# Giving out the middle stage's work in other portions, an earlier start for the second batch, and the order of w_in's quarters

## The chip, the core and the metric

The kernel runs on one core of a Trainium2 chip. The metric is the device time of one execution in microseconds (us). The kernel before took 2536.88 us (median of three runs, 2535.14 to 2537.12).

## The reference

```python
X = np.fft.rfft(x, axis=1)                       # x: 8 batches x 3008 x 256
Yr = Xr @ w_r - Xi @ w_i + b_r                   # 256 x 256, on every frequency
Yi = Xr @ w_i + Xi @ w_r + b_i
Yr = np.sign(Yr) * np.maximum(np.abs(Yr) - lam, 0.0)     # lam = 0.01, the same for Yi
y = np.fft.irfft(Yr + 1j * Yi, n=3008, axis=1)
h = y.reshape(24064, 256) @ w_in                 # 256 x 2048
out = np.maximum(0.01 * h, h) @ w_out            # 2048 x 256
```

w_in and w_out are drawn in double precision and are handed over as pairs of 32-bit words, from which the kernel makes its float numbers itself.

## The kernel before

**Tiling.** The length 3008 is 47 x 64, so the transform of a batch is done in matrix products in two passes. `fwd(b)` does the pass over 47 and writes `u_dram`. `mid(b)`, the middle stage, does the pass over 64, the projection with w_r and w_i, the threshold and the first pass back, and writes `v_dram`. `inverse` reads pieces of it (`vin`), does the last pass, and `forms` makes the operands of the MLP from its result. The MLP goes over 24064 tokens in 47 chunks of 512 tokens, with 8 steps (`q`) a chunk. `moe_a` and `moe_b` make the hidden layer with 7 products per block in place of 8 (L99), `moe_o` multiplies by w_out (L652). Behind the first batch, each product is three matmuls over operands split into a high and a low part (`_hi`, `_lo`).

**The middle stage.** It goes over 12 pairs of frequencies per batch. For the pair j:
- `stage_b(j)` (L379): 4 matmuls from the loaded `u`, and the split of the result into `eh` and `el` (L393 to L396).
- `proj(j)`: 6 matmuls with `wr` into one bank (`ps_k`), from which ACT copies `kc` (L415) and POOL makes `kb` (L417); then 6 with `wn` and 6 with `wd` into another (`ps_y`).
- the threshold on DVE (L425 `t`, L426 `c`, L427 `t`), four moves into `zf` on ACT (L431, L435), the split into `zh` on ACT (L442) and `zl` on DVE (L443).
- `stage_g(j)`: 3 matmuls of 512 columns with `gb`, the copy `v` on ACT (L458) and two DMAs to `v_dram` from ACT's queue (L460).

From the second batch on, every bank of these stages comes from a tag of two banks, `psf`, which `inverse` (L524, `psf<-ga,vin`) and `fwd` use too. For the first batch, nothing of the MLP is there to run beside; its middle stage is the startup.

**What sets the order.** `mid` and `fwd` are generators. Each yields how much work it has just given out, as columns of matmul. The main loop (L798 to L816) walks over the half steps of the MLP; before each it asks the streams to reach a share `frac` of their whole work. `Stream.to` (L702 to L715) takes pieces until the work given out reaches that; a yielded None ends the call, so that the next piece comes a half step later at the soonest. For the middle stage of the second batch (`cur == 0`) `frac` stays at zero for the first fifth of the way and then rises to 1. `tc.issue_after(ins)` places what is traced in its block behind `ins` in the issue order of the engine of `ins`; it adds no wait. Within these bounds a list scheduler chooses each engine's order. One middle stage has to end before the first `inverse` that reads it: that reads a mixed piece, whose `vin` tile has a half of the batch before and a half of this one (`v_load`, L509; the other loads are L503).

**The startup.** w_in comes in four quarters. `convert_win(c)` makes one quarter's float numbers (`float64_parts`: ACT L154 and L155, then DVE) and splits them in three casts on ACT (L196) with three subtractions on DVE (L197). It shares ACT and DVE with the first batch's middle stage.

Of the kernel before, what the change touches and what calls it, by code (L numbers as in the profile page):

```python
# [31 lines left out]
def spectral_mlp_kernel(  # L32
# [20 lines left out]
    D = w_r.shape[0]  # L53
# [7 lines left out]
    CS = 512  # L61
# [12 lines left out]
    sync, act, dve, pool = nc.sync, nc.scalar, nc.vector, nc.gpsimd  # L74

    def bank(tag, bufs):
        return ps.tile([P, 512], F32, name=tag, tag=tag, bufs=bufs)

    def products(dst, pairs):

        terms = []
        for l, r in pairs:
            terms += [(l[0], r[0]), (l[0], r[1]), (l[1], r[0])] if len(l) == 2 else [(l[0], r[0])]
        for i, (a, b) in enumerate(terms):
            last = nc.tensor.matmul(dst, a, b, start=(i == 0), stop=(i == len(terms) - 1))  # L85
        return last


    mlp = []
# [11 lines left out]
    def flat(t):  # L101
        return t.rearrange("p a b -> p (a b)")
# [46 lines left out]
    def float64_parts(raw, a, q):  # L149


        wl, wh = raw[:, :, 0], raw[:, :, 1]
        u = a.bitcast(U32)
        act.mul(q, wl, 2.0 ** -52)  # L154
        act.activation(a, wh.bitcast(F32), AF.Abs, scale=2.0 ** 16)  # L155
        dve.tensor_scalar(a, a, F64_MIN * 2.0 ** 16, F64_MAX * 2.0 ** 16, ALU.max, ALU.min)
        dve.tensor_scalar(u, u, 4, 1, ALU.logical_shift_left, ALU.logical_shift_right)
        dve.scalar_tensor_tensor(u, wh, 0x80000000, u, ALU.bitwise_and, ALU.bitwise_or)
        dve.tensor_scalar(wl, u, 0xFF800000, None, ALU.bitwise_and)
        dve.tensor_mul(q, q, wl.bitcast(F32))  # L160
# [3 lines left out]


    NIN = DF // 4
    win_raw = []

    def load_win(c, queues, behind=None):
        if c % 2 == 0:  # L170
# [9 lines left out]
    def convert_win(c):  # L180


        a, q, s = win_tmp
        if c == 3:
            a = sb.tile([P, NH * NIN], F32, name="cva", tag="wout_hi", bufs=1)
        float64_parts(win_raw[c], a, q)
        dve.tensor_add(a, a, q)
        a = a.rearrange("p (j q i m) -> p j q i m", j=NH, q=2, i=2)
        a11, a12, a21, a22 = (a[:, j, :, i] for i in range(2) for j in range(2))
        dve.tensor_add(s[:, 0], a21, a22)  # L190
        dve.tensor_sub(s[:, 2], a11, a21)
        dve.tensor_sub(s[:, 1], s[:, 0], a11)
        dve.tensor_sub(s[:, 3], a12, s[:, 1])
        hi, lo = (w[:, :, 2 * c:2 * c + 2] for w in consts["win"])
        for k, w in ((slice(0, 2), a[:, :, :, 0]), (2, a22), (slice(3, 7), s)):
            act.copy(hi[:, k], w)  # L196
            last = dve.tensor_sub(lo[:, k], w, hi[:, k].bitcast(F32))  # L197
        return last

# [36 lines left out]
    sent, reads, written, turned, turning, thresholded, filled, returned, tied = [], [], [], [], [], [], [], [], []  # L236
# [111 lines left out]
    def mid(b):  # L348
# [13 lines left out]
        def load(j):  # L362
            u = sb.tile([P, 2, D], F32, name="u", tag="u", bufs=3)
            for c in range(2):
                ld = sync.dma_start(u[c * N2:(c + 1) * N2], ud[c, 2 * j:2 * j + 2, :N2, :].rearrange("k n d -> n k d"))
                if b == 0:
                    reads.append(ld)
            u_t[j] = u
# [30 lines left out]
        def proj(j):  # L399

            e = e_t.pop(j)
            ps_k = bank("psf", 2) if b else bank("pso", 2)
            ps_y = None if b else bank("psf", 2)
            for dst, c, w in ((0, 2, "wr"), (0, 1, "wn"), (D, 0, "wd")):
                if c == 1 and b:
                    ps_y = bank("psf", 2)
                with tc.issue_after(mlp[0].ins) if b and c == 2 else nullcontext():
                    products((ps_k if c == 2 else ps_y)[:, dst:dst + D], [
                        (tuple(t[:, a, c, :] for t in e), tuple(t[:, a, :] for t in consts[w]) if b else (consts[w + "32"][0][:, a, :],)) for a in range(NH)
                    ])  # L410
                if c == 2:
                    kc = ps_k[:, :D]
                    if b:
                        kc = sb.tile([P, D + 40], F32, name="kc", tag="kc")[:, :D]
                        act.copy(kc, ps_k[:, :D])  # L415
                    kb = sb.tile([P, 2, D], F32, name="kb", tag="kb", bufs=1)
                    (pool if b else dve).tensor_add(kb, bias, kc.unsqueeze(1).broadcast_to([P, 2, D]))  # L417
                if c:
                    yield 6 * D
                if c == 2 and b and j:  # L420
                    stage_g(j - 1)
                    yield 3 * CS
            t = sb.tile([P, 2, D], F32, name="t", tag="t" if b else "v", bufs=1 if b else 2)
            c = sb.tile([P, 2, D], F32, name="c", tag="kb" if b else "yt", bufs=1)
            dve.tensor_add(flat(t), ps_y, flat(kb))  # L425
            dve.tensor_scalar(c, t, LAMBDA, -LAMBDA, ALU.min, ALU.max)  # L426
            thresholded.append(dve.tensor_sub(t, t, c))  # L427
            zf = z0[j % 3] if b == 0 else sb.tile([P, 2, D], F32, name="zf", tag="zf", bufs=1)
            for i in range(2):
                s = slice(64 * i, 64 * (i + 1))  # L430
                act.copy(zf[:64, i, :], t[s, 0, :])  # L431
                if b == 0 and j == NPAIR - 1:
                    dve.tensor_scalar(zf[64:, i, :], t[s, 1, :], sign[s, NK1 + j:NK1 + j + 1], None, ALU.mult)
                else:
                    act.mul(zf[64:, i, :], t[s, 1, :], sign[s, NK1 + j:NK1 + j + 1])  # L435
            if b == 0:
                z_t[j] = (zf,)
                yield 6 * D
                return
            z = sb.tile([P, 2, 2, D], F32R, name="zh", tag="z", bufs=1)  # L440
            zh, zl = z[:, 0], z[:, 1]
            act.copy(zh, zf)  # L442
            dve.tensor_sub(zl, zf, zh.bitcast(F32))  # L443
            z_t[j] = (zh, zl)
            yield 6 * D

        def stage_g(j):
            pg = bank("psh", 4) if b < 1 else bank("psf", 2)
            with tc.issue_after(filled[0].ins) if b == 0 and filled else nullcontext():
                last = products(pg, [(consts["gb" if b else "gb32"], tuple(flat(z) for z in z_t.pop(j)))])  # L450
            if b == 0:
                turning.append(last)
                tied[:] = [last]
                if NPAIR - 3 <= j < NPAIR - 1:
                    next(fp)
            v = sb.tile([P, 2, D], F32, name="v", tag="v" if b else "y") if b or j < NPAIR - 1 else sb.tile(
                [P, 2, D], F32, name="v", tag="t", bufs=1)
            act.copy(flat(v), pg)  # L458
            for c in range(2):
                put = act.dma_start(vd[c, 2 * j:2 * j + 2, :N2, :].rearrange("k n d -> n k d"), v[c * N2:(c + 1) * N2])  # L460
                if b == 0:
                    returned[:] = [put]
# [4 lines left out]
        if b:  # L467
            for s in range(NPAIR):
                if s + 2 < NPAIR:
                    load(s + 2)  # L470
                with tc.issue_after(mlp[0].ins):
                    stage_b(s)
                yield 16 * P
                yield None
                yield from proj(s)
            stage_g(NPAIR - 1)
            yield 3 * CS
            return
        for s in range(NPAIR + 3):
            if s + 2 < NPAIR:  # L480
# [319 lines left out]
    for i, pos in enumerate(moe()):  # L800
        if i % 2 == 0 and len(converted) < NQ:
            with tc.issue_after(made[0].ins), tc.issue_after(made[1].ins):
                next(wout, None)
        while cur + 1 < NB - 1 and pos >= (read[cur + 1] if cur >= 0 else 0):
            for s in streams:
                s.finish()
            cur += 1
            streams = ([Stream(fwd(cur + 1), (FWD + 4 * CS) * SHARE)] if cur else []) + [mids[cur]]
        frac = (pos - read[cur]) / (read[cur + 1] - read[cur]) if cur + 1 < NB else 1
        if cur == 0:  # L810
            frac = max(0, frac - 0.2) * 1.25
        work = frac / 0.95 * sum(s.total for s in streams)
        with tc.issue_after(converted[-1].ins) if cur == 0 else nullcontext():
            for s in streams:
                s.to(work / s.total)
                work = max(0, work - s.total)  # L816
# [106 lines left out]
```

## Time and profile before

| what | value |
|---|---|
| three runs | 2536.88, 2535.14, 2537.12 us |
| the profiled execution's own time | 2536.06 us |
| its span, first to last instruction | 2534.3 us |
| granted TensorE clock, mean | 0.996 |
| ACT L639, Prelu of 3/4 of a block | 368 times, 847 ns each |
| ACT L603, cast of a block | 376 times, 1050 ns each |

The table's first three rows are three measures of one thing: the execution that was profiled took 2536.06 us, of which 1.8 us lie around the span. A line of the profile reads "line engine operation out<-in"; names are those of the tiles, with buffer numbers left out. PE is TensorE's matmul, ACT is ScalarE, DVE is VectorE, POOL is GpSimd, SP is SyncE, whose queue carries most DMAs. A bracket at the end of a row of a timeline is the time for which the engine stood idle ahead of it, and what ended that.

### The profile page before, as it was taken

Reading aid. Unit: us, or ns where it says so; the run is one execution under the profiler, and the core shown is the slowest. Engines: PE = TensorE matmul, PEld = TensorE weight load, DVE = VectorE, ACT = ScalarE, POOL = GpSimd, SP = SyncE. Lnnn points to the kernel's source line nnn. Section 1 sums busy time; section 2 is a strip of 40 time slices with the busy share of each in tenths; the row PEclk is TensorE's granted clock in tenths of the full one; section 3 lists DMA queues with packets and bytes.
Section 4 is the critical chain, followed back from the end, with each engine's and each line's share of the span. In section 5 each row is a group of like instructions: output and inputs, shape, how many; then the busy total and the mean of one; then the engine's idle time right before and its main releaser. Section 6 shows DMA issues by size and latency. Waiting matters only on the chain.

```text
span 2534.3 us, 42321 instructions
## 1 busy us (share of the span) xinstructions
PE 2494.7 (98%) x16180; PEld 2246.1 (89%) x16180; DVE 1873.3 (74%) x3460; ACT 1661.8 (66%) x3152; POOL 122.2 (5%) x96
## 2 busy tenths in 40 slices
PE   5999999999999999999999999999999999999999
PEld 3688888999899998999989999899998999999998
DVE  6887787777877778777777777877778777667665
ACT  4776765767666765677666676666765677656564
POOL 0000000000000000000000000000000010000000
PEclk8999999999999999999999999999999999999999
DMA  8621132111321113221132111321113211100000
GB/s 263 201 79 50 46 93 78 48 50 45 96 73 51 54 39 91 69 58 50 42 95 69 51 51 41 103 69 54 43 38 113 64 54 42 42 21 29 21 14 17
DMA packets 117803, 165.05 MB, mean 65 GB/s; under 512 B 13513, under 2 KB 69345, under 8 KB 117601
## 3 DMA queue, kind: packets, MB, share of 16 engines
q1 hardware_dynamic: 76900, 115.09, 14.9%
q10 hardware_dynamic: 40701, 47.26, 7.4%
q8 instruction: 127, 2.08, 0.3%
q14 instruction: 75, 0.61, 0.1%
HBM read 86.59 MB, written 75.71 MB: 64 GB/s over the span
## 4 chain that ended last, share of the span: by engine, by line
PE 94%; DMA 2%; ACT 2%; DVE 1%; issue 0%; SPq 0%; ACTq 0%; DVEq 0%
PE pso L652 40%; PE psh L99 35%; PE psf L85 12%; PE psf L524 3%; PE psf L379 3%; DMA xin<-x_dram 1%; DMA u_dram<-xin 1%; PE psh L85 0%; DMA win_raw<-w_in_dram 0%; PE psh L379 0%; PE pso L85 0%; DVE gl L605 0%; ACT zf L435 0%; ACT xin L317 0%; ACT zf L431 0%
## 5 line engine op out<-in xcount | busy, mean ns | idle before, releaser
L99 PE MATMUL psh<-yh,win_hi 128*128 128x256 f32 (+1 forms) x2608 | 728.4, 281 | 0.9 <-DVE gf L636 0.4
L99 PE MATMUL psh<-yl,win_hi 128*128 128x256 f32 (+1 forms) x2608 | 728.5, 280 | 0.0
L99 PE MATMUL psh<-yh,win_lo 128*128 128x256 f32 (+1 forms) x2608 | 723.4, 279 | 0.0
L605 DVE TENSOR_TENSOR gl<-gf,gh 128x1024 fp32r<-128x1024 f32 x376 | 461.5, 1227 | 298.5 <-ACT gh L603 287.4
L652 PE MATMUL pso<-gh,wout_hi 128*128 128x512 f32 x1504 | 592.3, 394 | 0.5 <-ACT ob L657 0.5
L652 PE MATMUL pso<-gl,wout_hi 128*128 128x512 f32 x1504 | 589.8, 392 | 1.0 <-DVE gl L605 1.0
L652 PE MATMUL pso<-gh,wout_lo 128*128 128x512 f32 x1504 | 588.8, 391 | 0.0
L99 PEld LDWEIGHTS psh<-yh,win_hi 128*128 128x128 f32 x2608 | 488.5, 188 | 18.8 <-DVE gf L636 1.4
L99 PEld LDWEIGHTS psh<-yl,win_hi 128*128 128x128 f32 x2608 | 490.2, 188 | 16.8 <-DVE yl L551 0.3
L99 PEld LDWEIGHTS psh<-yh,win_lo 128*128 128x128 f32 x2608 | 488.9, 188 | 1.9
L639 ACT ACTIVATE gf<-gf 128x768 f32<-128x768 f32 x368 | 311.7, 847 | 215.7 <-DVE gf L636 204.5
L603 ACT CAST gh<-gf 128x1024 fp32r<-128x1024 f32 x376 | 394.8, 1050 | 34.5 <-PE pso L652 25.4
L652 PEld LDWEIGHTS pso<-gl,wout_hi 128*128 128x128 f32 x1504 | 282.4, 188 | 62.8 <-DVE gl L605 4.3
L652 PEld LDWEIGHTS pso<-gh,wout_hi 128*128 128x128 f32 x1504 | 282.7, 188 | 46.9 <-ACT ob L657 0.9
L652 PEld LDWEIGHTS pso<-gh,wout_lo 128*128 128x128 f32 x1504 | 282.6, 188 | 46.4
L638 ACT ACTIVATE gf<-psh 128x256 f32<-128x256 f32 x368 | 142.1, 386 | 233.4 <-PE psh L99 225.2
L636 DVE TENSOR_TENSOR gf<-psh,u 128x512 f32<-128x512 f32 x368 | 252.3, 686 | 47.1 <-PE psh L99 45.4
L620 ACT COPY p<-psh 128x256 f32<-128x256 f32 x368 | 137.5, 374 | 142.1 <-PE psh L99 131.2
L417 POOL TENSOR_TENSOR kb<-bias,kc 128x512 f32<-128x512 f32 x84 | 119.5, 1423 | 2046.6 <-ACT kc L415 1801.7
L621 DVE TENSOR_TENSOR u<-psh,p 128x256 f32<-128x256 f32 x368 | 154.5, 420 | 32.5 <-ACT p L620 30.4
L623 DVE TENSOR_TENSOR gf<-psh,u 128x256 f32<-128x256 f32 x368 | 154.7, 420 | 21.1 <-PE psh L99 7.4
L624 DVE TENSOR_TENSOR gf<-psh,gf 128x256 f32<-128x256 f32 x368 | 154.3, 419 | 4.9
(124 smaller groups left out, 3126.7 us busy)
## 6 DMA issues: line engine op xcount, KB each, us to landing
u<-u_dram SPq DMA_DIRECT2D x192, 128.0 KB, 2.7
v_dram<-v ACTq DMA_DIRECT2D x192, 128.0 KB, 2.4
out_dram<-ob SPq DMA_DIRECT2D x94, 256.0 KB, 2.0
vin<-v_dram SPq DMA_DIRECT2D x96, 240.0 KB, 3.5
xin<-x_dram SPq DMA_DIRECT2D x78, 240.0 KB, 3.0
u_dram<-xin ACTq DMA_DIRECT2D x72, 240.0 KB, 2.4
raw<-w_out_dram SPq DMA_DIRECT2D x8, 512.0 KB, 4.4
win_raw<-w_in_dram SPq DMA_DIRECT2D x7, 512.0 KB, 6.9
```

The lines of the kernel that those rows point to most:

```text
L85: last = nc.tensor.matmul(dst, a, b, start=(i == 0), stop=(i == len(terms) - 1))
L99: mlp[:] = [nc.tensor.matmul(dst, a, b, start=start and i == 0, stop=i == 2, skip_group_check=True)]
L603: cp = act.copy(gh, g)
L605: parted[:] = [cp, dve.tensor_sub(gl, g, gh.bitcast(F32))]
L620: act.copy(p1, b1[:, lo])
L621: dve.tensor_add(u2, b1[:, hi], p1)
L623: dve.tensor_add(g[:, 3], b2[:, hi], u2)
L624: dve.tensor_add(g[:, 3], b2[:, lo], g[:, 3])
L636: dve.tensor_add(g[:, 1:3], b2.rearrange("p (k n) -> p k n", k=2), u2.unsqueeze(1).broadcast_to([P, 2, HT]))
L638: act.activation(g[:, 0], b1[:, lo], AF.Prelu, alpha=SLOPE)
L639: act.activation(g[:, 1:4], g[:, 1:4], AF.Prelu, alpha=SLOPE)
L652: mlp[:] = [nc.tensor.matmul(po, a[:, f, s], r[:, i], start=(f == 0 and j == 0), stop=(f == NF - 1 and j == 2),)]
```

## The change

It has four parts. (1) `float64_parts` of a quarter of w_in is placed behind the last cast of the quarter before it on ACT. (2) From the second batch on, a pair's work is given out in three places: `stage_b`; the `wr` product with the previous pair's `stage_g`; the `wn` and `wd` products with the threshold. Each ends with None, and the pair's whole sum (18 D + 3 CS) is yielded once, after the threshold. Before, there were four yields of work in `proj` and a None only behind `stage_b`. The None behind the last pair stands before the last `stage_g`, which yields nothing now. (3) `stage_g` from the second batch on is placed behind the last matmul of the MLP. (4) The second batch's middle stage begins at 0.12 of its way instead of 0.2.

```diff
-    win_raw = []
+    win_raw, casts = [], []
...
-        float64_parts(win_raw[c], a, q)
+        with tc.issue_after(casts[-1].ins) if casts else nullcontext():
+            float64_parts(win_raw[c], a, q)
...
-            act.copy(hi[:, k], w)
+            casts.append(act.copy(hi[:, k], w))
...
-                if c:
+                if c and not b:
                     yield 6 * D
-                if c == 2 and b and j:
-                    stage_g(j - 1)
-                    yield 3 * CS
+                if c == 2 and b:
+                    if j:
+                        stage_g(j - 1)
+                    yield None
...
             z_t[j] = (zh, zl)
-            yield 6 * D
+            yield 18 * D + 3 * CS
 
         def stage_g(j):
...
-            with tc.issue_after(filled[0].ins) if b == 0 and filled else nullcontext():
+            with tc.issue_after((mlp if b else filled)[0].ins) if b or filled else nullcontext():
...
                 yield from proj(s)
+                yield None
             stage_g(NPAIR - 1)
-            yield 3 * CS
             return
...
         if cur == 0:
-            frac = max(0, frac - 0.2) * 1.25
+            frac = max(0, frac - 0.12) / 0.88
```

The program holds the same 15266 matmuls before and after. Line numbers of the changed kernel are one higher from L186 on and two higher from L427 on. Three places follow, as the program stands on an engine before and after.

**ACT at about 45 us**, where the casts of quarter 1 of w_in stand beside the first pairs of the first batch. `win_raw_251` is the raw data of quarters 2 and 3, `cva_725` belongs to quarter 3, `t_297` is the result of the first pair's threshold. Before:

```order
L196 CAST win_hi_178<-cva_180 128x2x256
L196 CAST win_hi_178<-cva_180 128x256
L154 ACTIVATE cvq_181<-win_raw_251 128x1024
L155 ACTIVATE cva_725<-win_raw_251 128x1024
L196 CAST win_hi_178<-ws_182 128x4x256
L155 ACTIVATE cva_180<-win_raw_251 128x1024
L431 COPY zf_230<-t_297 64x256
L435 ACTIVATE zf_230<-t_297,sign_111 64x256
```

After:

```order
L197 CAST win_hi_178<-cva_180 128x2x256
L197 CAST win_hi_178<-cva_180 128x256
L197 CAST win_hi_178<-ws_182 128x4x256
L154 ACTIVATE cvq_181<-win_raw_251 128x1024
L155 ACTIVATE cva_180<-win_raw_251 128x1024
L433 COPY zf_230<-t_297 64x256
L437 ACTIVATE zf_230<-t_297,sign_111 64x256
```

The last cast of quarter 1 moved ahead of both parts of quarter 2, and quarter 3's L155 (`cva_725`) left this place; it stands 33 rows later now, behind its L154.

**PE at about 300 us**, the end of a chunk, in the second batch's middle stage. `psf_2823` and, after, `psf_2842` are banks of `inverse`; `wr_hi,eh` is the `wr` product of a pair, `zh,gb` the `stage_g` of a pair before it. Before:

```order
L524 MATMUL psf_2823<-ga_256,vin_2696 128x128 x4
L99 MATMUL psh_2787<-yl_2261,win_hi_178 128x256
L99 MATMUL psh_2787<-yh_2260,win_lo_179 128x256
L99 MATMUL psh_2786<-yh_2260,win_hi_178 128x256
L99 MATMUL psh_2786<-yl_2261,win_hi_178 128x256
L99 MATMUL psh_2786<-yh_2260,win_lo_179 128x256
L85 MATMUL psf_2836<-wr_hi_201,eh_2763 128x256
L85 MATMUL psf_2836<-wr_lo_202,eh_2763 128x256
L85 MATMUL psf_2836<-wr_hi_201,eh_2763 128x256 x2
L85 MATMUL psf_2836<-wr_lo_202,eh_2763 128x256
L85 MATMUL psf_2836<-wr_hi_201,eh_2763 128x256
L85 MATMUL psf_2847<-zh_2715,gb_hi_213 128x512
```

After:

```order
L85 MATMUL psf_2786<-wr_hi_201,eh_2763 128x256
L85 MATMUL psf_2786<-wr_lo_202,eh_2763 128x256
L85 MATMUL psf_2786<-wr_hi_201,eh_2763 128x256 x2
L85 MATMUL psf_2786<-wr_lo_202,eh_2763 128x256
L85 MATMUL psf_2786<-wr_hi_201,eh_2763 128x256
L85 MATMUL psf_2797<-zh_2700,gb_hi_213 128x512
L526 MATMUL psf_2842<-ga_256,vin_2715 128x128 x4
L85 MATMUL psf_2797<-zh_2700,gb_hi_213 128x512
L85 MATMUL psf_2797<-zh_2700,gb_lo_214 128x512
L654 MATMUL pso_2964<-gh_2751,wout_hi_856 128x512
```

The four matmuls of `inverse` moved from ahead of the `wr` product to behind the first matmul of `stage_g`. On ACT, the long Prelu (L639 before, L641 after) moved at this place from behind the cast `zh` to a place ahead of it, and the copy `odd` of `inverse` from ahead of it to behind it.

**ACT at about 350 us**, where the second batch's middle stage ends. `v_3241` and, after, `v_3290` are the results of its last `stage_g`. Before:

```order
L620 COPY p1_3445<-psh_3431 128x256
L458 COPY v_3241<-psf_3237 128x512
L638 ACTIVATE gf_3375<-psh_3357 128x256
L460 DMA v_dram_1212<-v_3241 64x2x256 x2
L639 ACTIVATE gf_3375<-gf_3375 128x768
```

After:

```order
L622 COPY p1_3445<-psh_3431 128x256
L640 ACTIVATE gf_3375<-psh_3357 128x256
L641 ACTIVATE gf_3375<-gf_3375 128x768
L460 COPY v_3290<-psf_3286 128x512
L605 CAST gh_3464<-gf_3375 128x1024
L462 DMA v_dram_1116<-v_3290 64x2x256 x2
```

The copy and its two DMAs moved behind both Prelus, and the DMAs behind a cast too. On PE, 42 matmuls of the MLP stood between this `stage_g`'s last matmul and the first of `inverse` that reads its result (`vin_3343`); after the change 27 stand there, 6 of 512 columns and 21 of 256, with one of `fwd`. The middle stage of the second batch begins on PE 44 matmuls of the MLP sooner (behind 130 instead of 174), and its last matmul comes 21 later (behind 1038 instead of 1017).

## The prediction

> **What bounds the kernel now.** I read the page's first part (busy time and share of the span), then four windows by stage, then the waits of PE. A window's row has its bounds and length, the busy time of PE, weight loads, DVE, ACT and POOL (with counts), the granted clock, the DMA share and GB/s.
>
> ```profile
> PE 2494.7 (98%) x16180; PEld 2246.1 (89%) x16180; DVE 1873.3 (74%) x3460; ACT 1661.8 (66%) x3152; POOL 122.2 (5%) x96
> ```
> ```profile
> 0.00:135.00 135.00, 104.33 (x420) 71.23 (x421) 103.92 (x179) 86.56 (x165) 0.77 (x6) 0.92 0.74 222
> 135.00:500.00 365.00, 361.12 (x2342) 326.04 (x2341) 274.77 (x515) 244.00 (x473) 23.15 (x17) 1.00 0.23 66
> 500.00:2200.00 1700.00, 1699.68 (x11303) 1550.90 (x11303) 1277.48 (x2389) 1138.20 (x2198) 98.24 (x73) 1.00 0.22 61
> 2200.00:2534.30 334.30, 329.57 (x2121) 297.93 (x2119) 217.16 (x379) 193.07 (x319) 0.00 (x0) 1.00 0.06 19
> ```
>
> PE is the bound, at 98%. Of the windows' 2534.3 us it idles 39.6: 30.7 in the startup (135 - 104.33), 3.9 from 135 to 500, 0.3 from 500 to 2200, 4.7 in the last stretch. The change adds and removes no matmul, so it can only change idle time, or time at the low clock. In the 1700 us that hold the middle stages of the third batch and later there is 0.3 us to gain and any amount to lose. PE's waits say where the rest lies (what was waited for; us in total, times, longest):
>
> ```profile
> PE psh L379 <- ACT cva L155: 12.7, 1, 12.7
> PE psh L85 <- ACT zf L435: 3.0, 2, 2.7
> PE psf L85 <- ACT zh L442: 1.7, 1, 1.7
> PE pso L652 <- DVE gl L605: 1.0, 3, 0.5
> PE psf L85 <- ACT eh L395: 0.7, 1, 0.7
> PE psf L85 <- DVE y L530: 0.3, 1, 0.3
> ```
>
> The change reaches the 2.7 us on `zf` in the startup, and the waits on `zh` (1.7), `eh` (0.7) and `y` (0.3), all three in the second batch's middle stage. The 12.7 lies ahead of anything it moves.
>
> **The change part by part. (a) Quarter 1's last cast first.** The timelines of ACT, PE and DVE about 50 us (start, duration, in brackets the idling ahead of it):
>
> ```profile
> 50.45 1.12 ACT L155 ACTIVATE cva<-win_raw 128x1024 f32<-128x1024 f32 x1 [2.94 <-DMA win_raw<-w_in_dram]
> 51.47 1.04 ACT L196 CAST win_hi<-ws 128x1024 fp32r<-128x1024 f32 x1
> 53.44 0.39 ACT L431 COPY zf<-t 64x256 f32<-64x256 f32 x1
> 54.77 0.50 ACT L435 ACTIVATE zf<-t,sign 64x256 f32<-64x256 f32 x1
> 55.33 2.08 PE L85 MATMUL psh<-zf,w 128*128 128x512 f32 x2 [2.70 <-ACT zf L435]
> ```
> ```profile
> 48.94 0.42 DVE L193 TENSOR_TENSOR ws<-cva,ws 128x256 f32<-128x256 f32 x1
> ```
>
> ACT stands idle for 2.94 us until quarter 3's data land, with the cast of `ws` behind it, though `ws` is done at 48.94 + 0.42 = 49.36. After the change, the cast runs from 49.4, then quarter 2's L154 (at the 1.12 us of the L155 above) and L155 again, so 49.4 + 1.0 + 1.1 + 1.1 = 52.6; the four moves into `zf` take 55.27 - 53.44 = 1.83 and end at 54.4. PE resumes 0.9 us sooner than at 55.33. It doesn't gain all of that: the window rows put the clock at 0.70 from 50 to 60 and 0.96 from 60 to 70, which is the half clock from about 54.0 to 60.8.
>
> ```profile
> 50.00:60.00 10.00, 5.83 (x21) 4.42 (x22) 7.76 (x13) 8.37 (x14) 0.00 (x0) 0.70 0.69 208
> 60.00:70.00 10.00, 10.00 (x49) 8.19 (x49) 9.40 (x18) 6.99 (x14) 0.00 (x0) 0.96 0.66 188
> ```
>
> The pair of 512-column matmuls took 2.08 at 55.33 and takes 1.12 at full clock (98.41, below). What runs at half clock in 0.9 us is worth 0.45 at full clock, and PE is not idle from 60 to 70, so **-0.45**, from 0 (the next wait takes it) to -0.9.
>
> The Trainium skill, "TensorE: Matmul & The Clock Gate", section "Part 1: The HAM clock gate", says that the gate opens after one busy window of about 3.4 us, and that the window runs freely. Here the full clock came 60.8 - 55.3 = 5.5 us behind PE's restart, which lies between one window and two; by that rule an earlier restart may open the gate a window sooner. The sum goes by an unmoved 60.8.
>
> **(b) The startup's end.** Quarter 3's activations run later now, and on DVE the last pair's `kb` comes ahead of the last step of the pair before:
>
> ```profile
> 96.46 0.69 DVE L417 TENSOR_TENSOR kb<-bias,pso 128x512 f32<-128x512 f32 x1
> 98.41 1.12 PE L85 MATMUL psh<-zf,w 128*128 128x512 f32 x2 [0.27 <-ACT zf L435]
> ```
>
> PE already waits there, so up to 0.69 more can show; between 0 and 0.69 I take **+0.3**, since other matmuls (`fwd` of the second batch) lie on both sides of this wait.
>
> **(c) The second batch's pairs.** Of its three waits, those of 0.7 and 0.3 go, for their neighbours move apart: **-1.0**. In the new order two ends of a chunk have a pair's products and `inverse` in one row on PE, on two banks. A bank's next use there waits for `kc` or `t` to be read, with 0.9 us of other matmuls ahead. The price is like that of the two waits which went, between 0 and 0.74: I take 0.5 for each, **+1.0**.
>
> At 300 us the wait on `zh` stays and grows. The rows there:
>
> ```profile
> 299.23 1.05 PE L524 MATMUL psf<-ga,vin 120*128 120x128 f32 x8
> 303.26 0.50 PE L85 MATMUL psf<-zh,gb_hi 128*128 128x512 f32 x1 [1.72 <-ACT zh L442]
> ```
> ```profile
> 301.66 0.36 ACT L527 COPY odd<-psf 128x240 f32<-128x240 f32 x1
> 302.59 0.62 ACT L442 CAST zh<-zf 128x512 fp32r<-128x512 f32 x1
> 303.12 0.84 ACT L639 ACTIVATE gf<-gf 128x768 f32<-128x768 f32 x1
> ```
>
> The four matmuls of `inverse` (8 records, 0.9 us from start to end of their slots) stand behind `stage_g`'s first matmul now, so PE comes to the wait 0.9 sooner. On ACT the Prelu of 0.84 takes the place of `odd` (0.36) ahead of `zh`, so `zh` comes 0.5 later. 1.72 + 0.9 + 0.5 = 3.1, which is **+1.4**, from -1.72 (the threshold ends sooner as a whole) to +1.4.
>
> **(d) The handover of the second batch's result.** Before:
>
> ```profile
> 348.67 0.40 PE L85 MATMUL psf<-zh,gb_lo 128*128 128x512 f32 x1
> 350.65 0.39 PE L652 MATMUL pso<-gh,wout_hi 128*128 128x512 f32 x1
> 350.88 0.28 PE L99 MATMUL psh<-yh,win_hi 128*128 128x256 f32 x1
> 350.99 0.28 PE L99 MATMUL psh<-yl,win_hi 128*128 128x256 f32 x1
> 355.38 0.83 PE L524 MATMUL psf<-ga,vin 120*128 120x128 f32 x6
> ```
> ```profile
> 349.62 0.60 ACT L458 COPY v<-psf 128x512 f32<-128x512 f32 x1
> 350.25 1.24 ACTq L460 DMA_DIRECT2D v_dram<-v  x2
> ```
> ```profile
> 352.71 0.33 SPq L509 DMA_DIRECT2D vin<-v_dram  x1
> 353.54 0.41 SPq L509 DMA_DIRECT2D vin<-v_dram  x1
> DMA to landing us min/median/max: 2.0/2.5/3.0
> ```
>
> From the last `stage_g` matmul's start (348.67) to the two `vin` issues it is 4.04 and 4.87 us, and they land 2.0 and 3.0 later (two issues: the smallest and the largest value; I take the second for the slower): 6.0 and 7.9. `v` began 0.95 after that start, where the matmul itself takes 0.40; if ACT is free at its end, the chain is about 0.5 shorter: 5.5 and 7.3. PE had 355.38 - 348.67 = 6.71 us of other work between, then six records on the first half of `vin`, and no wait. A step of 512 columns is 0.23 and one of 256 is 0.115 by the rows above. After the change there are 6 x 0.23 + 21 x 0.115 + 0.23 for `fwd` + 0.23 for `stage_g`'s own matmul = 4.25 us, and the four matmuls of `inverse` end 0.9 later, at 5.1. The second half of `vin` is wanted by the last two of them, at about 4.7 to 4.9; it is there at 7.3: **+2.4**, from 0 (ACT's order lets `v` out sooner, or other matmuls slip between) to +3.4 (ACT's Prelu of 0.84 ahead of `v` counts in full).
>
> **(e) Other edits.** The `issue_after` in `stage_g` adds an order, no wait. On SP the second batch's first `u` loads now stand ahead of the last early load of w_out:
>
> ```profile
> u<-u_dram SPq DMA_DIRECT2D x192, 128.0 KB, 2.7
> ```
>
> Its data come up to 2.7 us later, and w_out's conversion has no reader near; 0. For the third to the eighth batch (72 pairs) I take 0: their span of 1700 us idles 0.3 now, and what is moved there keeps its cover of MLP matmuls. The ends are -0.3 and the slow rival's price below.
>
> **The sum** is -0.45 + 0.3 - 1.0 + 1.0 + 1.4 + 2.4 = +3.65 us against the profiled execution's 2536.06, so 2539.7. The median of the three runs is 0.82 above that execution, so I forecast **2540.5** against 2536.88.
>
> **The rivals.**
>
> *The new order brings waits in every later batch (slower).* A pair's threshold is given out with its projection now, so DVE gets it as one block:
>
> ```profile
> 97.25 0.69 DVE L425 TENSOR_TENSOR t<-psf,kb 128x512 f32<-128x512 f32 x1
> 97.98 0.43 DVE L426 TENSOR_SCALAR c<-t 128x512 f32<-128x512 f32 x1
> 98.44 0.69 DVE L427 TENSOR_TENSOR t<-t,c 128x512 f32<-128x512 f32 x1
> ```
>
> That is 1.81 us in which no `gl` (L605) is made, and PE already waits for `gl` at three places (1.0 in all, above). For it: DVE is busy 75% of the stretch, the highest of the helpers. Against it: in 1700 us the present order shows 0.3 of idling. It decides if `gl` comes late by 0.1 to 0.2 at each of 72 pairs: +7 to +14, which gives 2547.5 to 2554.5.
>
> *The new waits don't come (no change).* The three waits of (c) go, 2.7 together, and (d) is hidden. For it: a pair has a half step between each of its three parts now, so `zh` should have been ready long before `stage_g`; against it: at 300 us the order still has `stage_g` right behind the `wr` product. -0.45 + 0.3 - 2.7 gives 2534.0; with (d) at half its price, 2535.2.
>
> *The gate opens sooner.* If the clock follows PE's restart by 3.4 us at the soonest (54.4 + 3.4 = 57.8 for 60.8), up to 3.0 us of half clock go, worth 1.5: 2539.0. The page of the skill named above has this rule. The rows of this trace have 5.5 us, so I hold it unlikely.
>
> **How the numbers follow.** Forecast 62% (2537 to 2544), the gate 6% (2539.0), no new waits 17% (2534 to 2537), waits in every batch 15% (2547.5 to 2554.5). The range leaves out most of the slow rival and the lower edge of the other: 2534.5 to 2546. About 0.2% (5.1 us) is what a measurement of this kernel can tell from no change, so the bounds are 2531.8 and 2542.0. Above 2542.0 lie the slow rival (15%) and the upper part of the forecast, 16%: slower 31%. Below 2531.8 only a gain that I can't name: 5%. The rest, 64%, is the same.
>
> **What would show it.** (a) PE's wait on `zf` at 52 us shrinks from 2.7 to about 1.8. (c) The waits on `eh` and `y` at 241 us are gone; PE's wait on `zh` at 300 us is about 3.1; (d) a wait of 2.4 us on `vin` stands ahead of `inverse` near 356 us. PE's idle time from 500 to 2200 us stays under 1 us; several us there mean the slow rival. A time under 2535 with no wait at 356 us would prove (d) wrong.

## The result, and the profile after

The changed kernel took 2557.53 us (median of four runs, 2553.27 to 2562.59) against 2536.26 us: 1.0086 times as long (95% interval 1.0074 to 1.0099). It is slower by 21 us where the prediction had 4, and its runs lie 9 us apart, those of the kernel before 2 us.

The head of the profile of the changed kernel, and its waits of PE that are new or larger:

```profile
PE 2506.1 (98%) x16180; PEld 2253.9 (88%) x16180; DVE 1876.8 (73%) x3460; ACT 1660.9 (65%) x3152; POOL 118.5 (5%) x96
```
```profile
PE pso L654 <- DVE gl L607: 4.6, 4, 1.5
PE psh L99 <- DVE gf L638: 3.1, 3, 2.4
PE psf L85 <- ACT zh L444: 2.5, 1, 2.5
PE psf L526 <- DMA vin<-v_dram: 1.8, 2, 1.5
PE pso L654 <- ACT ob L659: 1.4, 1, 1.4
PE psf L85 <- DVE xz L282: 1.0, 1, 1.0
```

PE idles for 48.9 us of the 2555.0 (39.6 before), 9.3 more. Its busy time grew too, by 11.4 us, with the same number of matmuls: part of the loss is in the clock. Windows by stage, before and then after (bounds, length, busy PE, weight loads, DVE, ACT, POOL, then the granted clock):

```profile
290.00:345.00 55.00, 53.28 (x367) 49.11 (x366) 38.76 (x72) 38.43 (x79) 5.48 (x5) 1.00 0.16 44
345.00:400.00 55.00, 54.13 (x326) 47.33 (x325) 48.04 (x94) 30.00 (x55) 0.00 (x0) 1.00 0.45 127
640.00:760.00 120.00, 120.00 (x771) 108.32 (x770) 92.86 (x178) 73.36 (x134) 1.30 (x1) 1.00 0.31 87
760.00:2150.00 1390.00, 1389.68 (x9252) 1268.16 (x9251) 1043.76 (x1953) 931.90 (x1804) 82.78 (x62) 1.00 0.22 61
2150.00:2300.00 150.00, 150.00 (x983) 136.59 (x982) 105.29 (x189) 93.04 (x163) 2.00 (x1) 1.00 0.11 32
```
```profile
290.00:345.00 55.00, 52.18 (x335) 46.71 (x334) 37.48 (x68) 35.24 (x71) 5.45 (x5) 0.94 0.16 44
345.00:400.00 55.00, 52.50 (x313) 45.78 (x312) 45.16 (x85) 30.70 (x57) 0.00 (x0) 0.97 0.42 115
640.00:760.00 120.00, 114.52 (x718) 102.45 (x717) 90.47 (x173) 71.45 (x132) 1.29 (x1) 0.99 0.31 88
760.00:2150.00 1390.00, 1388.26 (x9231) 1267.30 (x9230) 1038.69 (x1941) 923.36 (x1786) 79.79 (x61) 1.00 0.21 61
2150.00:2300.00 150.00, 148.20 (x974) 134.80 (x973) 103.98 (x189) 95.25 (x176) 3.88 (x3) 1.00 0.11 33
...
302.00:309.00 7.00, 6.12 (x18) 4.72 (x19) 2.54 (x4) 2.98 (x8) 1.27 (x1) 0.51 0.22 65
363.60:367.00 3.40, 3.34 (x9) 2.20 (x9) 2.69 (x7) 2.06 (x5) 0.00 (x0) 0.50 0.52 154
705.00:708.40 3.40, 3.02 (x14) 3.03 (x15) 1.31 (x4) 1.89 (x2) 0.00 (x0) 0.51 0.28 72
```

The reader is to see three things. Idle time stands where there was none, in the stretches 640 to 760 (5.5 us) and 2150 to 2300 (1.8). In three places the clock falls to half in the middle of the kernel, for 6.8, 3.4 and 3.4 us; 1.1 us of that lie inside waits, and half of the rest, 6.3 us, is lost. And the stretch from 760 to 2150, the longest by far, idles 1.4 us more only, so most of the loss is not spread over the pairs.

The same account can be made in finer grain. For each of PE's matmuls, take the distance from its start to the next one's start, less the median distance in the kernel before between two matmuls of these shapes; the sum over a stretch is the **time lost** there. It holds idle time, half clock and waits too short for the view. Against the kernel before, in us (profiled executions; the last column is the sum, and the changes of the spans agree with it within 1.7 us):

| kernel | 0-130 | 130-290 | 290-345 | 345-400 | 400-640 | 640-760 | 760-2150 | 2150- | sum |
|---|---|---|---|---|---|---|---|---|---|
| the change | 0.0 | -0.9 | +4.6 | +3.2 | +0.4 | +7.9 | +3.0 | +3.3 | +21.5 |
| pace92 | -0.3 | -0.7 | -1.8 | +1.0 | -0.2 | +0.8 | +6.1 | +0.2 | +5.1 |
| start20 | -1.5 | -2.2 | +2.0 | +7.6 | +0.3 | +10.7 | +3.4 | +3.3 | +23.6 |
| second_end | -1.9 | -0.7 | -1.9 | +0.6 | +0.4 | +5.1 | +2.3 | +3.0 | +6.9 |
| third_end | -0.8 | -0.9 | +4.5 | +2.9 | -0.2 | +2.0 | +3.0 | +3.2 | +13.8 |
| vin_pool | +2.3 | -0.9 | +3.5 | +3.9 | +0.4 | +4.2 | +1.0 | +2.7 | +17.1 |
| xin_u | -0.9 | -0.8 | +2.2 | +3.4 | +0.5 | +3.5 | +5.2 | +3.8 | +16.9 |
| fold_pool | -0.9 | -0.8 | +3.6 | +1.8 | +0.5 | +4.0 | -0.9 | +4.5 | +11.8 |
| old_pace94 | -0.8 | 0.0 | +3.3 | +1.7 | -0.2 | -0.1 | +6.3 | +0.5 | +10.6 |
| old_pace98 | -1.5 | -0.5 | -0.7 | +1.1 | -0.4 | +4.7 | +6.9 | +0.7 | +10.4 |
| early_rise | -1.1 | -0.1 | -1.8 | +0.2 | -0.1 | 0.0 | +0.9 | 0.0 | -2.0 |
| old_start12 | +1.4 | +2.7 | -2.1 | +2.7 | -0.2 | -0.1 | 0.0 | +0.1 | +4.6 |
| casts_only | -0.6 | +1.6 | 0.0 | 0.0 | +0.1 | 0.0 | +0.7 | 0.0 | +1.9 |
| pace92_start20 | -1.6 | 0.0 | +4.7 | +0.9 | -0.3 | +0.8 | +3.9 | +0.4 | +8.8 |
| old_xin_u | -0.4 | 0.0 | 0.0 | +0.1 | +0.1 | +0.8 | +3.9 | +0.1 | +4.6 |

One profile is one execution, and it need not be the median one: that of xin_u is of its fastest run, 5.6 us under its median, that of second_end of its fastest, 2.4 us under.

**What became later.** On PE, the distance between a batch's last `stage_g` and the first `inverse` that reads it, in matmuls of the MLP, shrank in three batches: from 42 to 27 in the second, from 87 to 48 in the third, from 74 to 9 in the eighth. The fourth to the seventh have 105 to 107 in both. Followed through the generators, the last `stage_g` of a batch is given out two half steps of the MLP later in the second to the seventh batch, and one later in the eighth. A pair now counts the 3 CS of a `stage_g` that only the next pair gives out, so that each later pair begins behind its old share of the way; and behind the last pair the whole sum has been counted, and a None stands, before its `stage_g` comes. The fourth to the seventh batch are shifted by the same two half steps and keep their distance on PE; why the scheduler's order gives way in the others is not shown.

### The profile page after: what moved, and what is told of

The parts are those of the page before. It is cut to its first block, busy times and chain, and to the rows that moved or that the text cites. A ratio compares the mean times of both kernels' runs of the same rounds, so it can differ in the third digit from the quotient of the medians.

```text
span 2555.0 us, 42273 instructions
## 1 busy us (share of the span) xinstructions
PE 2506.1 (98%) x16180; PEld 2253.9 (88%) x16180; DVE 1876.8 (73%) x3460; ACT 1660.9 (65%) x3152; POOL 118.5 (5%) x96
## 3 DMA queue, kind: packets, MB, share of 16 engines
q8 instruction: 127, 2.08, 0.3%
## 4 chain that ended last, share of the span: by engine, by line
PE 90%; DMA 3%; ACT 3%; DVE 2%; issue 1%; SPq 0%; ACTq 0%; POOL 0%; DVEq 0%; POOLq 0%
PE pso L654 39%; PE psh L99 34%; PE psf L85 11%; PE psf L526 3%; PE psf L380 3%; DMA xin<-x_dram 1%; DMA u_dram<-xin 1%; DMA win_raw<-w_in_dram 1%; PE psh L85 0%; DVE gl L607 0%; DMA vin<-v_dram 0%; ACT zf L437 0%; DVE gf L638 0%; ACT zf L433 0%; ACT gf L641 0%
## 5 line engine op out<-in xcount | busy, mean ns | idle before, releaser
L99 PEld LDWEIGHTS psh<-yh,win_hi 128*128 128x128 f32 x2608 | 489.5, 188 | 23.6 <-DVE gf L638 4.4
L641 ACT ACTIVATE gf<-gf 128x768 f32<-128x768 f32 x368 | 311.8, 847 | 216.1 <-DVE gf L638 207.8
L418 POOL TENSOR_TENSOR kb<-bias,kc 128x512 f32<-128x512 f32 x84 | 115.9, 1379 | 2074.4 <-ACT kc L416 1848.3
```

The costliest lines, as they stand in the source:

```text
L99: mlp[:] = [nc.tensor.matmul(dst, a, b, start=start and i == 0, stop=i == 2, skip_group_check=True)]
L641: act.activation(g[:, 1:4], g[:, 1:4], AF.Prelu, alpha=SLOPE)
```

## The experiments

All times are medians of four runs or more, beside runs of the kernel before on the same chip. The names "Theory 1" and so on are those of the expectations.

### pace92: all middle stages end sooner

```diff
-        work = frac / 0.95 * sum(s.total for s in streams)
+        work = frac / 0.92 * sum(s.total for s in streams)
```

> The changed kernel with the streams' pace divided by 0.92 instead of 0.95, so that each middle stage ends sooner: between a batch's last stage_g and the first inverse that reads it stand 42, 88 and 60 matmuls of the MLP for the second, third and eighth batch (27, 48 and 9 in the changed kernel, 42, 87 and 74 before), and the row of wr product, stage_g and inverse at 300 us is gone. Theory 1 (the late end of the middle stages costs: about 3 us at 360, 8 at 670 to 710, 3 at 2217; the row at 300 us another 4): 2537 to 2541. Theory 2 (a pair in three places is itself dearer, wherever it ends): 2550 or more. Theory 3 (only the row at 300 us matters, by the clock it loses there and later): 2553.

2540.28 us against 2536.81 (ratio 1.0011, 1.0002 to 1.002). With the early ends, and without the row at 300 us, 17 of the 21 us are back, and with pairs still in three places: theory 3 falls, and theory 2 as the main cause. The stretches 640 to 760 and 2150 on are back to +0.8 and +0.2. It is not quite the kernel before: 3.5 us stay, and its profile loses 6.1 from 760 to 2150, half of it in waits of 0.9 to 1.1 us on `gl` and `gf` at 1321, 1344 and 1632 us, though its ends there are early. What these come from, three places or other rows, is not shown.

### start20: the second batch begins at 0.2 again

```diff
-            frac = max(0, frac - 0.12) / 0.88
+            frac = max(0, frac - 0.2) * 1.25
```

> The changed kernel with the second batch's middle stage begun at 0.2 again. The row at 300 us is gone in the program, and only 8 matmuls of the MLP are left between the second batch's last stage_g and the first inverse behind it (27 in the changed kernel); the third and the eighth batch stay at 48 and 9. Theory 1 (late ends cost): 4 us go at 300, 2 to 4 come at 360, the rest stays: 2555 to 2558. Theory 2 (three places are dearer): 2553 to 2558, with the loss spread over the span. Theory 3 (only 300 us): 2537 to 2541.

2555.96 (1.0075, 1.0063 to 1.0088). The row at 300 us is gone and 2.6 us with it, but with 8 matmuls left behind the second batch's end, 345 to 400 lost 7.6 us in place of 3.2. The time is nearly the same, so the early start is not what the 21 us come from.

### second_end and third_end: one batch at a time

```diff
-            frac = max(0, frac - 0.12) / 0.88
+            frac = max(0, frac - 0.12) / 0.85
```

> The changed kernel, where only the second batch's share rises faster (divided by 0.85, not 0.88), so that it alone ends as early as before (42 matmuls of the MLP behind its last stage_g) and the row at 300 us is gone; the third and the eighth batch keep their late ends (48 and 9). Theory 1: the 4.6 and 3.2 us lost at 290 to 345 and 345 to 400 go, the 7.9 at 640 to 760 and the 3.1 at 2150 to 2300 stay: 2549 to 2552. If the losses of the third batch come from what the second set off (a shift of everything by some us): they go too, 2540 to 2544.

2544.52 (1.0045, 1.0033 to 1.0057), 13 us less than the changed kernel. The losses of 290 to 400 us are gone (-1.9 and +0.6), those at 640 and 2150 stay (+5.1, +3.0), as theory 1 has it. The time fell by 5 us more than expected and lies between the two cases, so it is the stretches that speak for theory 1, and third_end below. In this profiled execution the clock stayed at full from 57 us to the last matmuls, so its +5.1 holds no half clock.

```diff
-        work = frac / 0.95 * sum(s.total for s in streams)
+        work = frac / (0.92 if cur == 1 else 0.95) * sum(s.total for s in streams)
```

> The changed kernel, where only the streams of the third batch are paced by 0.92: 88 matmuls of the MLP stand behind its last stage_g (48 in the changed kernel), the second and the eighth batch keep 27 and 9, and the row at 300 us stays. If its late end causes the loss at 640 to 760: that 7.9 goes to 0 to 1, the 4.6, 3.2 and 3.1 elsewhere stay: 2548 to 2551. If it comes from a shift that the second batch set off: 2555 to 2558.

2549.38 (1.0047, 1.0035 to 1.006): 8 us less, as expected, most of it at 640 to 760, where 7.9 fell to 2.0, with the other places as in the changed kernel. The third batch makes its own loss, by its late end or by a row that moved with it: the pace shifts all of its pieces.

### What carries the third batch's late end to PE

In the changed kernel, the waits of PE at 640 to 760 us are for DVE. DVE's queue at the three of them, and PE behind them:

```profile
677.28 0.69 DVE L273 TENSOR_TENSOR xs<-xin,xin 120x512 f32<-120x512 f32 x1 [2.47 <-DMA xin<-x_dram]
677.89 1.22 DVE L607 TENSOR_TENSOR gl<-gf,gh 128x1024 fp32r<-128x1024 f32 x1
...
691.61 0.68 DVE L553 TENSOR_TENSOR yl<-yt,yh 128x512 fp32r<-128x512 f32 x1
692.21 0.42 DVE L282 CAST xz<-xin 120x512 fp32r<-120x512 f32 x1
692.55 0.68 DVE L553 TENSOR_TENSOR yl<-yc,yh 128x512 fp32r<-128x512 f32 x1
693.15 1.22 DVE L607 TENSOR_TENSOR gl<-gf,gh 128x1024 fp32r<-128x1024 f32 x1
...
704.03 0.69 DVE L273 TENSOR_TENSOR xs<-xin,xin 120x512 f32<-120x512 f32 x1 [1.31 <-DMA xin<-x_dram]
704.64 0.68 DVE L638 TENSOR_TENSOR gf<-psh,u 128x512 f32<-128x512 f32 x1
```
```profile
679.16 0.50 PE L654 MATMUL pso<-gl,wout_hi 128*128 128x512 f32 x1 [1.54 <-DVE gl L607]
...
694.42 0.50 PE L654 MATMUL pso<-gl,wout_hi 128*128 128x512 f32 x1 [1.50 <-DVE gl L607]
...
705.38 0.58 PE L99 MATMUL psh<-yh,win_hi 128*128 128x256 f32 x1 [2.45 <-DVE gf L638]
```

At 677 us DVE stands before a fold (`xs`, the first step of the next batch's forward pass) whose x has not landed, for 2.47 us, with `gl` behind it. At 693 it doesn't wait at all: `gl` stands behind the forms of the next chunk (`yl`) and the forward pass's splits. At 704, the longest of the three, a fold waits for x again, with `gf` behind it. A fold that waits for x is not new: in the kernel before, one does so for 2.83 us at the same time, and PE idles for none of it.

```profile
704.26 0.69 DVE L272 TENSOR_TENSOR xs<-xin,xin 120x512 f32<-120x512 f32 x1 [2.83 <-DMA xin<-x_dram]
```

Three kernels ask which of these matters: another queue for the `vin` loads that stand ahead of x on SP, another buffer for x, or the folds off DVE.

```diff
-                ld = sync.dma_start(vin[:, c, :, :], vv[c, :, s:s + 2, :])
+                ld = q.dma_start(vin[:, c, :, :], vv[c, :, s:s + 2, :])
...
-                sync.dma_start(vin[:, c, i, :], vv[c, :, s_, :])
+                q.dma_start(vin[:, c, i, :], vv[c, :, s_, :])
```

(`q` is `pool` for a pair that is mixed or begins a batch, else `sync`.)

> The changed kernel with the first two vin loads of each new batch issued from POOL's queue instead of SP's; the ends of the middle stages stay late. Theory 1a (behind the third batch's end, SP waits for v with the next batch's first xin load queued behind it, DVE waits for xin, and gl behind that): the waits at 677 to 703 us shrink, 8 us there become 0 to 3, the second batch's places stay: 2549 to 2554. Theory 1b (the late end itself sets the time, by whichever queue vin is loaded): no change, 2555 to 2560.

2550.16 (1.0057, 1.0044 to 1.0069). The time is that of theory 1a, but 7.9 fell to 4.2 where it wanted 0 to 3, and the test is not clean: a load of a further pair kept its place on SP ahead of x, and DVE still stood up to 3.1 us before a fold (2.5 in the changed kernel). The third batch's distance went from 48 to 54 matmuls too.

```diff
-                    sb.tile([PA, 2 * D], F32, name=f"xin{h}", tag="uv"[h], bufs=3 - h)[:, :n] for h in range(2)
+                    sb.tile([PA, 2 * D], F32, name=f"xin{h}", tag=t, bufs=3 if t == "u" else 2)[:, :n]
+                    for h, t in enumerate("uu" if c == 1 else "uv")
```

> The changed kernel, where the second pair of x loads of a batch (from the fourth on) takes a buffer of the u tiles for its other half too, in place of the buffer of the last v. Theory 1c (the last v comes late, its buffer is wanted by xin, DVE waits for xin ahead of gl): the 7.9 us lost at 640 to 760 shrink to 0 to 3, and the losses ahead of 400 us stay: 2549 to 2553. Theory 1b (what counts is that the end and the next batch's beginning lie close on PE and ACT): 2555 to 2560.

> The kernel before with the same choice of buffer, nothing else. Its ends are early, and PE hardly waits behind 400 us: 2534 to 2537 by theory 1c, for there is nothing to gain. If it is above 2539, the third u buffer was wanted by something else.

xin_u took 2557.63 (1.0086, 1.0073 to 1.0099), no gain, which is theory 1b's range, and old_xin_u 2541.11 (1.0022, 1.0013 to 1.003), 5.5 us slower than the kernel before. The choice holds from the third batch on. It does what it says at one place: the fold that waited 2.47 waits for nothing now. But later folds wait 2.1 and 1.8 in its place, and PE loses 3.5 there, in an execution whose clock stayed at full, and 5.2 from 760 to 2150 us. This buffer doesn't bring x soon enough, and a third user of the u buffers has a price of its own: old_xin_u idles 3.6 us from 760 to 2150, nearly all on `gl` and `gf` near 1010, 1320 and 1945 us.

```diff
-            eng = dve
+            eng = pool if b >= NPRE else dve
```

> The changed kernel with the folds of x (two adds for each pair of x tiles, from the third batch's forward pass on) on POOL instead of DVE; ends as late as in the changed kernel. If DVE's queue carries the loss (the fold's wait for xin, and 1.4 us of folds per pair of tiles ahead of gl): the gl waits at 640 to 760 fall from 5.5 us of idling to 0 to 1.5, and 7.9 goes to 0 to 3: 2549 to 2553. If it is carried by ACT or by PE's own order: 2555 to 2559.

2545.38 (1.0032, 1.002 to 1.0044), 12 us less than the changed kernel, with ends as late as there. Its waits of PE from 640 to 760 us:

```profile
PE pso L654 <- DVE gl L607: 0.8, 1, 0.8
PE psh L99 <- DVE gf L638: 0.7, 1, 0.7
PE psh L99 <- DVE gf L626: 0.3, 1, 0.3
```

Against 3.0 on `gl` and 2.4 on `gf` in the changed kernel. So DVE's queue carries the late end to PE: folds that wait for x, and folds as such, ahead of `gl` and `gf`. About half of the loss there is shown by this: 4.0 of the 7.9 stay (0 to 3 expected), 2.1 of idling and short waits. All of these waits are for DVE, and part of them POOL brought with it: the `gl` at 693 and 701 us took 1.99 and 2.34 us while POOL's folds ran, 1.22 elsewhere. The gain in all is larger than expected, since the stretch from 760 to 2150 lost nothing any more (-0.9 in place of +3.0).

### The kernel before, with one part

```diff
-        work = frac / 0.95 * sum(s.total for s in streams)
+        work = frac / 0.94 * sum(s.total for s in streams)
```

> The kernel before with its pace divided by 0.94 instead of 0.95, nothing else. On PE this gives the second batch the row at 300 us that the changed kernel has (wr product, one matmul of stage_g, four of inverse, the rest of stage_g) and its short end (27 matmuls of the MLP behind the last stage_g); the third to the eighth batch keep the ends of before (87 to 108, and 74). Theory 1 (those two places cost 4 and 3 us, the third and eighth batch's late ends the rest): 2542 to 2545, with nothing lost behind 400 us. If the second batch's places set off the losses of the later batches too: 2550 or more. If three places per pair are what costs: 2536 to 2538.

2550.14 (1.0053, 1.004 to 1.0065), slower than expected by 5 us and more. What was expected came: 2.54 us of idling at 300 us and 0.98 twice at 360, a loss of 5.0 up to 400 us. But 6.3 more were lost from 760 to 2150, where the ends are as early as before:

```profile
PE pso L652 <- DVE gl L605: 3.5, 5, 1.1
PE psh L99 <- DVE gf L636: 2.0, 2, 1.5
```

These are the same two waits for DVE, and at three of them a fold stands ahead that waited for x (for 1.65 us until 1010, 1.70 until 1325, 2.08 until 1945). So a late end is not the only way in which the boundary of two batches goes wrong: a pace that moves the pieces by a half step gives other rows there, and some of them put `gl` behind what isn't ready. The expectation's second case, that the second batch's places set off the later losses, fits this time as well. Against it stands second_end, where the second batch loses nothing and the later losses stay; the run itself doesn't tell the two apart. In the kernel before, PE idles 0.3 in this stretch.

```diff
-        work = frac / 0.95 * sum(s.total for s in streams)
+        work = frac / 0.98 * sum(s.total for s in streams)
```

> The kernel before, its pace divided by 0.98 instead of 0.95, nothing else: the second batch keeps 42 matmuls of the MLP between its last stage_g and the first inverse behind it, the third to the seventh have 55 (87 to 107 before), the eighth 41 (74 before). Theory 1: what 48 did to the third batch, 55 does in part to five batches: 3 to 6 us each, 2551 to 2566. Theories 2 and 3: as before, 2535 to 2539.

2546.91 (1.004, 1.0026 to 1.0053), 10 us slower with late ends in the kernel before, and less than the 14 us and more of theory 1. The third batch (55 matmuls) lost 4.7 in place of the 7.9 that 48 cost; how much of the 6.9 behind it is due to the ends is not settled, after old_pace94.

```diff
-            frac = max(0, frac - 0.2) * 1.25
+            frac = max(0, frac - 0.12) / 0.88
```

> The kernel before with only the second batch's earlier start (0.12): its ends are not later (54 matmuls of the MLP behind the second batch's last stage_g, 42 before), the row of wr product, stage_g and inverse at 300 us is gone, and one of 31 matmuls stands at the chunk's end near 180 us. Theory 1: 2534 to 2537. Theory 3 (an early start makes rows that cost the clock): 2540 or more.

2540.81 (1.0015, 1.0006 to 1.0023), 4 us slower and not faster, although the end is early (54 matmuls), which is theory 3's case: a wait of 2.1 on `gf` at 372 us with half clock behind it, and waits of 1.1, 1.0 and 0.9 in rows of the second batch.

> The kernel before with only the order of w_in's quarters. The prediction's term is -0.45 to -0.9 us in the startup: 2535.5 to 2537. If PE's restart some tenths sooner shifts the clock's return too: up to 1.5 us less, 2534.5.

(The diff is the change's first part.) 2535.32 against 2536.14 (0.9999, 0.999 to 1.0008): no difference.

### Two mixtures

> The changed kernel with the pace divided by 0.92 and the second batch begun at 0.2: ends as early as before (45, 88, 104 to 138, 60 matmuls of the MLP behind the last stage_g), and the pairs in three places. What is left against the kernel before is the three places and the order of the quarters. Theory 1: 2535 to 2540. If three places cost by themselves: 2541 or more.

(The edits of pace92 and start20 together.) 2546.18 (1.0039, 1.0025 to 1.0053). Its ends are early, and yet it is 6 us slower than pace92, and theory 1's range is missed: a `wr` product waits 3.8 us for `eh` at 301 us, and the clock is at half for 6.8 us from 303 us on. A row of products, not an end, is what costs here, as at 300 us in the changed kernel. The expectation's second case is not shown by it: pace92 has the three places too.

```diff
-            frac = max(0, frac - 0.2) * 1.25
+            frac = max(0, frac - 0.15) / 0.85
```

> The kernel before with the order of the quarters, and the second batch's share begun at 0.15 and divided by 0.85: on PE, that batch's pairs keep the early end (42 matmuls of the MLP), and the row at 300 us is gone; everything behind 400 us is as before. From second_end, which had the same rows there: -2 us at 130 to 400 us: 2533 to 2535. If an early begin costs by itself: 2537 to 2541, as old_start12.

2534.67 against 2536.93 (0.9993, 0.9984 to 1.0001), with the order of the quarters as in the change. It has the lowest median of all these kernels, but the interval reaches 1, so a gain is not shown. Its profile has 1.8 us less lost at 290 to 345, since PE's wait on `zh` at 300 us is gone. So an earlier start of the second batch may be worth up to 2 us, if its pairs fall beside the chunk's ends and its last one stays early.

## Why the prediction was wrong

**The step that failed is (e):** "For the third to the eighth batch (72 pairs) I take 0: their span of 1700 us idles 0.3 now, and what is moved there keeps its cover of MLP matmuls." That span and the end behind it lost 14.2 of the 21.5 us (7.9 + 3.0 + 3.3). The cover was not kept: of the 87 and 74 matmuls of the MLP behind the ends of the third and the eighth batch, 48 and 9 were left, and in (d) only the second batch's end was priced. third_end, with 88 again, takes 5.9 of the third batch's 7.9 away, and fold_pool shows that DVE's queue carries at least 3.9 of that loss: it wasn't `vin` itself that came late for PE there, which is all that a sum of the handover's chain can see, but the next batch's forward pass and the next chunk's forms, which fall on DVE at one time ahead of `gl`.

**A second term was left out: the clock behind a wait.** The prediction weighed the clock in the startup only. Its two long waits cost more by that:

- (c) at 300 us it foresaw 3.1 of waiting. The wait was 2.54 (from 1.72). From 0.6 us ahead of its end the clock was at half for 6.8 us, of which about 3.1 are lost: +4.6 in place of +1.4.

```profile
302.80 0.79 PE L85 MATMUL psf<-zh,gb_hi 128*128 128x512 f32 x1 [2.54 <-ACT zh L444]
```

- (d) it foresaw 2.4 on `vin`. On `vin` PE waits 1.46. The 0.98 ahead of it are for a split of the forward pass (`xz`), which was not foreseen; that the two make 2.4 is luck only in part, for without the first PE would have come to `vin` so much sooner. The old 0.45 behind them shrank to under 0.1; with 3.4 us of half clock it came to +3.2.

```profile
360.69 0.50 PE L85 MATMUL psf<-xz,fa_hi 120*120 120x512 f32 x1 [0.98 <-DVE xz L282]
363.31 0.56 PE L526 MATMUL psf<-ga,vin 120*128 120x128 f32 x2 [1.46 <-DMA vin<-v_dram]
```

The mechanism was right in (c), and in (d) for `vin`, and the lengths nearly so; their price lacked the clock.

**(a)** fell, without weight. The cast of `ws` does stand first now, but DVE made `ws` 0.9 us later. Its order from `kb` (L418) to `ws` is that of before, but this `kb` waited 0.41 us for PE and began at 45.46 instead of 44.53, and PE was behind: its granted clock from 40 to 43 us was 0.54, where it was 0.95.

```profile
49.88 0.42 DVE L194 TENSOR_TENSOR ws<-cva,ws 128x256 f32<-128x256 f32 x1
```
```profile
50.33 1.04 ACT L197 CAST win_hi<-ws 128x1024 fp32r<-128x1024 f32 x1 [4.32 <-DVE ws L194]
...
54.73 0.50 ACT L437 ACTIVATE zf<-t,sign 64x256 f32<-64x256 f32 x1
```

`zf` is done at 55.23, as before (55.27), and PE's wait on it was 2.79, not 1.8. The step took the end of `ws` from the old trace (49.36); in this execution it came later, behind a PE whose clock rose later. **(b)** held: the wait at 98 us grew from 0.27 to 0.74, by 0.5 where 0.3 was taken. In **(c)** the waits of 0.7 and 0.3 went, and the 0.5 each that were to take their place came to 0.37 and 0.13.

**The rivals.** The slower rival gave the size (11 to 18 us over the kernel before; it was 21) and named the wait, `gl` late on DVE, but not its place: it wanted 0.1 to 0.2 at each of 72 pairs, from a block of 1.81 us on DVE. Such a spread is not there: 19.0 of the 21.5 us lie at 300 us and where one batch ends and the next begins (near 360, at 640 to 760, and from 2150 on). So the idling from 500 to 2200 us, 7.3 us, which the prediction took as this rival's sign, has another cause. The rival "the gate opens sooner" was about the startup, where no time was won (0.0); the gate mattered by closing.

**What stays open.** From 760 to 2150 us the changed kernel lost 3.0, though its ends there are as early as before; fold_pool shows that DVE's queue carries that too, but not which of the moved pieces began it. The loss at 2150 on (9 matmuls left) was undone only together with the others, by pace92. third_end moved all pieces of the third batch and not its end alone, and fold_pool took work off DVE, so neither parts the late end from the rows that come with it. The row at 300 us stands without half clock in one profile, that of xin_u: there the same 2.54 us come with a loss of 2.2 at 290 to 345, in place of 4.6.

## What to carry to other kernels

When work is given out in larger portions and counted only when it is done, look at the last portion: its successor's slack shrinks (here from 87 to 48 matmuls, and from 74 to 9), and the price can come in on the queue that holds the next stage's first steps ahead of the steady work. Price a changed order at every boundary of its kind, not at the one where the change shows first, and compare the distances there (in instructions of the engine that bounds) before and after. And a wait of PE of 2 us and more can have two prices here: its length, and half of a stretch of 3.4 or 6.8 us at the low clock.

## What the runs showed of the hardware

A short idling of PE in the middle of the kernel can halve its clock, for about 3.4 us or twice that, and the same idling need not. In the profiled executions, idle stretches of 2.45 us (the changed kernel at 703), 2.5 (old_pace98 at 683) and 2.1 (old_start12 at 372) were followed by half clock for 3.4 us (at 703 from 0.4 us ahead of the stretch's end), and 3.84 (pace92_start20 at 301) by 6.8, from 1.3 us ahead of its end; single stretches of 1.5 (the changed kernel at 677 and 693) and 1.7 (the kernel before at 301) by none. The same 2.54 us at 300 us was followed by 6.8 us of half clock in the changed kernel and third_end, by 3.4 in old_pace94 and vin_pool, and by none in xin_u. Even 0.74 and 0.31 us at 240 us, which stand in the kernel before without a trace in the clock, were followed by 3.4 us of half clock in casts_only. The page "TensorE: Matmul & The Clock Gate" of the Trainium skill, in "Part 1: The HAM clock gate", has a window of about 3.4 us that runs freely: the lengths here agree with it, and a window that doesn't follow PE's work would fit the chance. Of the idle stretches above that were followed by half clock, all but the 3.84 are shorter than such a window. The spread of the runs goes with the clock in one kernel: xin_u's four runs had a mean clock of 0.997, 0.994, 0.994 and 0.993 and took 2552.07, 2556.25, 2559.01 and 2560.07 us. The changed kernel, with several waits of 1 to 3 us, varies by 9 us in four runs, the kernel before by 2 in four and by 5 in 21.

In fold_pool, DVE's `gl` took 1.99 and 2.34 us at 693 and 701 us, where adds of 120x512 ran on POOL at the same time, and 1.22 in the mean where none did.
